# A fixed order for the value and sum matmuls of a fused attention and MoE kernel

## The chip, the cores and the metric

The kernel runs on one core of one Trainium2 chip. The metric is device time in microseconds (us). The kernel before has a median of 995.36 us over three runs (995.13 to 997.5).

## The reference, cut to what matters

```python
scores = scale * q @ k.T                       # batch 4, 8 heads, 768 positions, 64 wide
scores = where(mask, scores, -1e9)             # neighbours, first and last block, 3 sampled blocks
attn = exp(scores - max(scores))               # per row
attn = attn / (sum(attn) + 1e-9)
x = (attn @ v) -> [3072 tokens, 512]           # 8 heads side by side
h = x @ w_in                                   # 512 -> 2048
g = where(h >= 1, h, where(h <= -1, 0, (h + 1)**2 / 4))
out = g @ w_out                                # 2048 -> 512
```

Everything is float32, and the two weights arrive as 64-bit numbers.

## The kernel before, in words

The work is cut into 32 visits (one head of one batch each) and into MoE passes over half a batch (384 tokens), 16 steps of 128 hidden units per pass. A visit works on 6 column blocks `c` of 128 keys and two halves `hf` of 384 queries:

- `max_mm` (L285): 12 matmuls that recompute the scores once in one pass to find each row's maximum. DVE reduces each result (`max_red`, L291), takes the larger of two (L296), and PE transposes the column of maxima into a row (`max_turn`, L302, 6 small matmuls). ACT writes the row, negated, into row 96 of the query tile (`max_row`, L307), so that the score matmul subtracts it.
- `scores` (L323, L324): per block and half two matmuls into one PSUM bank; ACT takes the exponential (`expo`, L328) into a tile `pt`.
- `values` (L345): 12 matmuls of `pt` with `lv`. Each is a full float32 matmul, which the trace shows as two instructions. Its output is 64 rows wide: the half `hf` says whether it lands in rows 0 to 63 or 64 to 127 of the bank, so two neighbours use different halves of the array's columns.
- the row sums. In the first batch, whose visits the code calls `wide`, PE makes them: `p_tot` (L368), 12 float32 matmuls with a matrix of ones, 32 rows wide, in four column strips; ACT copies them out (L376) and they go through DRAM (`r_in`, `r_den`, `recip`) to come back as `den` for `x_mul` (L412). In the later batches POOL adds the tiles up (`p_sum`, L337), and `acc_sum` (L358) reduces them on DVE.
- `x_hi`, `x_lo` (ACT L224, DVE L422) split x into two reduced-precision parts for the MoE.

A MoE step is 12 matmuls `l1` (L487 to L489), an activation chain over ACT and DVE, and 9 matmuls `l2` (L521 to L523). The MoE of a batch starts when its 8 heads are done, and is mixed with the attention of the next batch. In the first 300 us or so the weights are converted as well: 16 conversions, each an ACT operation, four DVE operations over 1024 columns (L197 to L202), and two ACT casts with two DVE subtractions (L209).

What sets the order: every operation is entered into a list with a due time (`at`), in units of which one visit has 12 and with offsets from the tables `P`, `PW` and `PM`. The list is sorted and recorded in that order. The framework's scheduler then makes each engine's program from the recorded operations: it keeps the dependencies, but an instruction may stand before or behind one that was recorded earlier. Each engine executes its program strictly in order. SP issues nearly all transfers, in its own order.

Buffers: PSUM ring `pa` has three banks, used by `max_mm` (and by the scores of the later batches); scores of the first batch rotate over `oa0`, `oa1` and `hp`; 14 `pt` tiles; two sets of query and key tiles.

Of the kernel before, what the change touches and what calls it, by code (L numbers as in the profile page):

```python
# [38 lines left out]
def body(ctx, tc, qk_t, v, sampled_blocks, moe_w_in, moe_w_out, ind, cm, ident, fold, out):  # L39
    nc = tc.nc  # L40
    pool = lambda name, bufs, **kw: ctx.enter_context(tc.tile_pool(name=name, bufs=bufs, **kw))
    cst = pool("cst", 1)
    ld = pool("ld", 1)
# [6 lines left out]
    mt = pool("mt", 2)  # L50
# [98 lines left out]
    def after(key, *needs):  # L149
        assert all(x in passed for x in needs), (key, needs)  # L150
        passed.add(key)

    def at(t, fn, *args):
        plan.append((t, fn, args))

    turns = {}

# [15 lines left out]
    def plan_conversions():  # L173
        last = 1e9
        for t, load, bits, splits in sorted(conv, key=lambda x: -x[0]):
            last = t = min(t, last - P["cd"] * 2)
            at(t - P["cl"], load)
            at(t, bits)
            for i, split in enumerate(splits):
                at(t + P["cs"] + i * P["cg"], split)  # L180

    def convert(t, src, parts):
        st = {}

        def load():
            st["raw"] = cv.tile([128, 1024, 2], I32, name="raw", bufs=2)
            w = 1024 // len(src)
            for n in range(len(src)):
                Q_RAW.dma_start(out=st["raw"][:, n * w:(n + 1) * w],
                                in_=src[n].bitcast(I32).rearrange("p (c w) -> p c w", w=2))  # L190

        def bits():
            raw = st["raw"]
            lo32, hi32 = raw[:, :, 0], raw[:, :, 1]
            a = st["a"] = cv.tile([128, 1024], I32, name="cva", bufs=2)
            nc.scalar.activation(out=f(a), in_=f(hi32), func=AF.Abs)
            nc.vector.tensor_scalar(out=f(a), in0=f(a), scalar1=CLO, scalar2=CHI, op0=ALU.max, op1=ALU.min)  # L197
            nc.vector.tensor_scalar(out=a, in0=a, scalar1=3, scalar2=0x3FFFFFFF,
                                    op0=ALU.logical_shift_left, op1=ALU.bitwise_and)
            nc.vector.scalar_tensor_tensor(out=a, in0=hi32, scalar=-0x40000000, in1=a,  # L200
                                           op0=ALU.bitwise_and, op1=ALU.bitwise_or)
            nc.vector.scalar_tensor_tensor(out=a, in0=lo32, scalar=29, in1=a,  # L202
                                           op0=ALU.logical_shift_right, op1=ALU.bitwise_or)

        def split(cols, dst, done):
            a = f(st["a"])[:, cols]
            hi, lo = dst()
            rounded(CH, hi, a)
            nc.vector.tensor_tensor(out=lo, in0=a, in1=f(hi), op=ALU.subtract)  # L209
            done()  # L210

        conv.append((t, load, bits, [lambda x=x: split(*x) for x in parts]))
# [13 lines left out]
    def visit(n, b, h, pst):  # L226
# [3 lines left out]
        wide = n < H  # L230
        G = {**P, **PW} if wide else {**P, **PA} if n < 2 * H else P
        o0 = (L, R)[e]
# [77 lines left out]
        for m, (t, kh) in enumerate(jobs):  # L310
            u = n0 - (G["m0"] - G["m1"] * m / len(jobs))
# [118 lines left out]
                    at(s + G["ps"], p_sum, hf, c)  # L430
        for g in range(T // VG):
            u = n0 + 2 * (g + 1) * VG - 1 + G["lag"]
            at(u, values, g)
        for hf in range(2):
            at(u + G["ot"], o_copy, hf)
        if wide:
            at(u + 0.01, p_tot)
            at(u + G["al"], p_row)
            if e:
                y = u + G["su"]  # L440
                at(y, r_in)
                at(y + G["de"], r_den)
        else:
            at(n0 + 2 * T - 1 + G["al"] + G["ps"], acc_sum)
# [17 lines left out]
    def moe(t0, p, b, hf, fis, new=()):  # L462

        g = {}
        G = {**P, **PM} if new else P
        first, final = fis[0] == 0, fis[-1] == NF - 1
# [5 lines left out]
        def w_dst(fi):  # L472
            w = g["w", fi] = wst.tile([128, 2, DM], F32R, name="w")
            return w[:, 0], w[:, 1]

        def w_keep(fi):
            Q_KEEP.dma_start(out=f(wo_dram[fi]), in_=f(g["w", fi].rearrange("p a d -> p (a d)")))
# [75 lines left out]
        for i, fi in enumerate(fis):  # L553
            u = t0 + i * p
            if fi in new:
                if fi % 2 == 0:
                    convert(u + 1.5 * p - P["co"], [moe_w_out[k * 128:(k + 1) * 128, :] for k in (fi, fi + 1)],
                            [(slice((k - fi) * 512, (k - fi) * 512 + 512), lambda k=k: w_dst(k), lambda k=k: (w_keep(k), after(("wo", k))))
# [22 lines left out]
    at(-97, mask)  # L581
    at(-PW["qs"] + 0.1, mask_copies)
    at(-PW["qs"] + 0.15, mask_rest)
    for n in range(B * H):
        b, h = divmod(n, H)
        if h % 2 == 0:
            pst = {}
        visit(n, b, h, pst)
    full = tuple(range(NF))
    low, high = full[:NF // 2], full[NF // 2:]  # L590
    t = PER * H + D0
    for hf, fis, new in ((0, low, low), (1, full, high), (0, high, ())):
        moe(t, STEP0, 0, hf, fis, new)
        t += STEP0 * len(fis)
    for k in range(2, 2 * B):
        moe(PER * H * (1 + k / 2) + DELAY, PER * H / 2 / NF, k // 2, k % 2, full)
    for q in range(4):
        for kp in range(2):
            cs = slice(q * 512, (q + 1) * 512)
            u = 2 * q + kp  # L600
            convert(PER * H + D0 + (u - 4) * CSTEP - CONV + (STEP0 * NF / 2 if u > 3 else 0), [moe_w_in[k * 128:(k + 1) * 128, cs] for k in (2 * kp, 2 * kp + 1)],
                    [(slice((k % 2) * 512, (k % 2) * 512 + 512), lambda k=k, cs=cs: (wi[:, k, 0, cs], wi[:, k, 1, cs]),
# [1 line left out]
    plan_conversions()  # L604
    plan.sort(key=lambda x: x[0])
    for _, fn, args in plan:
        fn(*args)


LV, PT, VG, XT = 3, 14, 6, 10  # L610
STEP0 = 2.598
D0 = 10.127
P = {'r2': 3.428, 'qs': 8.321, 'vs': 2.922, 'ld': 2.0, 'm0': 7.7, 'm1': 5.1, 'mr': 0.037, 'mc': 2.3, 'mt': 1.061, 'mw': 0.459, 'ex': 0.5, 'ps': 0.823, 'lag': 0.994, 'ot': 0.4, 'al': 0.6, 'su': -0.02, 'de': 0.459, 're': 0.77, 'xm': -0.138, 'xh': 0.6, 'xl': 1.0, 'gr': 0.1, 'gs': 0.28, 'gm': 0.31, 'gh': 0.98, 'gl': 1.16, 'l2': 1.5, 'l3': 0.153, 'l1': 0.128, 'cl': 8.824, 'cs': 1.971, 'cd': 1.02, 'co': 5.155, 'cg': 1.066}
PW = {'qs': 9.6, 'vs': 4.0, 'ld': 4.0, 'm0': 9.0, 'm1': 8.0, 'mr': 0.3, 'mc': 0.9, 'mt': 0.6, 'mw': 0.373, 'ex': 0.6, 'ps': 1.084, 'lag': 1.153, 'ot': 0.4, 'al': 0.827, 'su': 1.75, 'de': 4.297, 're': 4.434, 'r2': 3.0, 'xm': -2.06, 'xh': 0.635, 'xl': 1.0}
PA = {}
PM = {'gr': -0.015, 'gs': 0.186, 'gm': 0.437, 'gh': 1.095, 'gl': 1.403, 'l2': 1.518, 'l3': 0.158, 'l1': 0.13}
RINGS = {"s": ("oa0", "oa1", "hp"), "m": ("pa", "pa")}
DELAY = 6.457
SETS = 2
PER = 2 * T  # L620
CONV = 4.0
CSTEP = 5.599
CLO, CHI = (struct.unpack("<f", struct.pack("<I", w))[0] for w in (0x38100000, 0x47EFFFFF))

_INS = ["qk_t", "v", "sampled_blocks", "moe_w_in", "moe_w_out"]
# [47 lines left out]
```

## Time and profile before

| | before |
|---|---|
| median of 3 runs | 995.36 us |
| profiled execution | 997.67 us |
| its span, first to last instruction | 995.9 us |
| PE busy | 971.9 us, 98% |
| PE weight loads busy | 764.5 us, 77% |
| DVE, ACT, POOL busy | 540.6, 527.9, 257.5 us |

The profiled execution is 2.3 us above the median, and 1.8 us longer than its span. Matmuls are pipelined: in the trace one lasts longer than the distance to the next, so the table's 98% says that PE always had something in flight, not that it ran at its shortest distances.

### The profile page before, as it was taken

How to read it: one execution, taken by the hardware profiler on the slowest of the kernel's cores; microseconds unless marked ns; L12 is line 12 of the kernel's file. 1: busy time of each engine (PE TensorE's matmuls, PEld its weight loads, DVE VectorE, ACT ScalarE, POOL GpSimd, SP SyncE). 2: the span in 40 equal slices, each digit the busy share in tenths (PEclk: the TensorE clock that was granted, in tenths of full speed). 3: DMA queues.
4: the chain of work that ended last, by engine and by line, in shares of the span. 5: the costliest groups of instructions: out<-in, count | busy, mean ns of one | idle time of the engine just before them, and what ended most of it. 6: DMA issues, size and time to landing. Idle time of an engine off the chain costs nothing.

```text
span 995.9 us, 13899 instructions
## 1 busy us (share of the span) xinstructions
PE 971.9 (98%) x5018; PEld 764.5 (77%) x5018; DVE 540.6 (54%) x918; ACT 527.9 (53%) x1043; POOL 257.5 (26%) x253
## 2 busy tenths in 40 slices
PE   5999999999999999999999999999999999999998
PEld 2444544578878898688888888888888888899997
DVE  5666754599878655654545556554545553322222
ACT  3546644557656555455555555555555545433433
POOL 1000000534332432533333344333333344000000
PEclk9999999999999999999999999999999999999999
DMA  6655664457774555545555545555555523433432
GB/s 210 166 157 166 164 183 136 118 182 249 236 221 134 163 179 171 162 136 156 154 153 163 160 124 150 166 151 156 157 152 166 149 86 101 154 127 127 159 126 96
DMA packets 53941, 155.99 MB, mean 157 GB/s; under 512 B 9130, under 2 KB 13386, under 8 KB 53872
## 3 DMA queue, kind: packets, MB, share of 16 engines
q1 hardware_dynamic: 53768, 154.93, 52.3%
q8 instruction: 40, 0.66, 0.3%
q14 instruction: 29, 0.24, 0.1%
q10 hardware_dynamic: 104, 0.17, 0.1%
HBM read 101.70 MB, written 15.61 MB: 118 GB/s over the span
## 4 chain that ended last, share of the span: by engine, by line
PE 88%; DVE 5%; DMA 4%; ACT 2%; issue 1%; SPq 0%; ACTq 0%
PE po L345 12%; PE oa L521 8%; PE oa L522 8%; PE oa L523 8%; PE hp L487 7%; PE hp L488 7%; PE hp L489 7%; PE pa L285 7%; PE pa L323 5%; PE pa L324 5%; PE oa L345 3%; DMA qk<-in_qk_t_dram 2%; DVE mc L291 2%; PE oa L323 2%; PE oa L368 1%; PE oa L324 1%
## 5 line engine op out<-in xcount | busy, mean ns | idle before, releaser
L337 POOL TENSOR_TENSOR acc<-acc,pt 128x384 f32<-128x384 f32 x192 | 201.2, 1049 | 217.4 <-ACT pt L328 214.5
L291 DVE TENSOR_REDUCE mc<-pa 128x1 f32<-128x384 f32 x384 | 203.4, 552 | 83.4 <-PE pa L285 77.4
L328 ACT ACTIVATE pt<-pa 128x384 f32<-128x384 f32 x288 | 140.5, 491 | 129.8 <-PE pa L324 121.6
L502 DVE SCALAR_TENSOR_TENSOR r<-r,hp 128x384 f32<-128x384 f32 x112 | 61.7, 551 | 203.7 <-ACT r L498 203.7
L487 PE MATMUL hp<-x,wi 128*128 128x384 f32 x448 | 153.0, 342 | 0.8 <-DVE r L502 0.7
L521 PE MATMUL oa<-w,gh 128*128 128x512 f32 x384 | 151.5, 395 | 0.3 <-ACT gh L224 0.3
L488 PE MATMUL hp<-x,wi 128*128 128x384 f32 x448 | 151.6, 338 | 0.0
L523 PE MATMUL oa<-w,gl 128*128 128x512 f32 x384 | 151.6, 395 | 0.0
L522 PE MATMUL oa<-w,gh 128*128 128x512 f32 x384 | 151.4, 394 | 0.0
L489 PE MATMUL hp<-x,wi 128*128 128x384 f32 x448 | 150.9, 337 | 0.0
L337 POOL TENSOR_TENSOR acc<-pt 128x384 f32<-128x384 f32 x48 | 52.6, 1097 | 360.0 <-ACT pt L328 196.8
L345 PE MATMUL po<-pt,lv 128*64 128x384 f32 x672 | 133.0, 496 | 0.0
L285 PE MATMUL pa<-KA,QA 88*128 88x384 f32 x384 | 128.8, 364 | 4.1 <-DMA QA<-qkh 2.2
L513 DVE TENSOR_TENSOR gl<-r,gh 128x384 fp32r<-128x384 f32 x128 | 89.7, 700 | 50.1 <-ACT gh L224 49.2
L494 ACT ACTIVATE r<-hp,half_c 128x384 f32<-128x384 f32 x112 | 65.0, 580 | 73.3 <-PE hp L489 71.9
L323 PE MATMUL pa<-QA,KA 97*128 97x384 f32 x288 | 101.8, 353 | 1.7 <-DVE mc L291 0.7
L285 PEld LDWEIGHTS pa<-KA,QA 88*128 88x128 f32 x384 | 71.3, 192 | 38.8 <-DVE mc L291 27.6
L324 PE MATMUL pa<-QB,KB 128*128 128x384 f32 x288 | 97.7, 339 | 0.0
L345 PEld LDWEIGHTS po<-pt,lv 128*64 128x64 f32 x672 | 55.3, 137 | 47.6 <-issue 40.1
L487 PEld LDWEIGHTS hp<-x,wi 128*128 128x128 f32 x448 | 84.6, 189 | 7.1 <-DVE r L502 3.9
L224 ACT CAST gh<-r 128x384 fp32r<-128x384 f32 x128 | 65.7, 513 | 40.8 <-DVE r L502 40.2
L488 PEld LDWEIGHTS hp<-x,wi 128*128 128x128 f32 x448 | 84.4, 188 | 1.8 <-DVE x L422 0.9
(85 smaller groups left out, 1222.4 us busy)
## 6 DMA issues: line engine op xcount, KB each, us to landing
w<-wo_dram SPq DMA_DIRECT2D x112, 512.0 KB
qk<-in_qk_t_dram SPq DMA_DIRECT2D x32, 384.0 KB
raw<-in_moe_w_in_dram SPq DMA_DIRECT2D x16, 512.0 KB
raw<-in_moe_w_out_dram SPq DMA_DIRECT2D x16, 512.0 KB
wo_dram<-w SPq DMA_DIRECT2D x16, 512.0 KB
lv<-in_v_dram SPq DMA_DIRECT2D x32, 192.0 KB
KA<-qkh SPq DMA_DIRECT2D x32, 192.0 KB
QA<-qkh SPq DMA_DIRECT2D x32, 192.0 KB
```

The lines of the kernel that those rows point to most:

```text
L285: nc.tensor.matmul(out=pm[:, 0:HALF], lhsT=QAi[0:KM, t * 128:(t + 1) * 128], rhs=KAi[0:KM, kh * HALF:(kh + 1) * HALF], start=True, stop=True)
L291: nc.vector.reduce_max(out=st["mc"][:, t, kh:kh + 1], in_=st.pop(("pm", t, kh))[:, 0:HALF], axis=AX.X)
L323: nc.tensor.matmul(out=ps[:, 0:HALF], lhsT=KAi[0:97, ks], rhs=QAi[0:97, cs], start=True, stop=False)
L324: nc.tensor.matmul(out=ps[:, 0:HALF], lhsT=st["KB"][:, ks], rhs=st["QB"][:, cs], start=False, stop=True)
L337: nc.gpsimd.tensor_tensor(out=st["acc"][:, hf], in0=prev, in1=st["p", hf, c], op=ALU.add)
L345: nc.tensor.matmul(out=st["po"][(L, R)[hf], 0:HALF], lhsT=st["lv"][:, c], rhs=st["p", hf, c], start=(c == 0), stop=(c == T - 1))
L487: nc.tensor.matmul(out=hv, lhsT=wi[:, j, 0, fs], rhs=x[:, 0], start=(j == 0), stop=False)
L488: nc.tensor.matmul(out=hv, lhsT=wi[:, j, 0, fs], rhs=x[:, 1], start=False, stop=False)
L489: nc.tensor.matmul(out=hv, lhsT=wi[:, j, 1, fs], rhs=x[:, 0], start=False, stop=(j == NP - 1))
L521: nc.tensor.matmul(out=o, lhsT=gh[:, ts], rhs=w[:, 0], start=(fi == fis[0]), stop=False)
L522: nc.tensor.matmul(out=o, lhsT=gh[:, ts], rhs=w[:, 1], start=False, stop=False)
L523: nc.tensor.matmul(out=o, lhsT=gl[:, ts], rhs=w[:, 0], start=False, stop=(fi == fis[-1]))
```

## The change

Three helpers are added. `behind` gives the scheduler an order without a semaphore: this instruction after that one. `fenced` records a function, chains all its PE instructions one behind the other, and puts the first behind the last 6 PE instructions recorded before. `traced` puts the first 10 PE instructions recorded behind a fenced group after that group's last. `values` and `p_tot` are now recorded through `fenced`, and all due times are new: the loads and splits of a first-batch visit (`qs`) are due 12.35 units ahead instead of 9.6, its maxima (`m0`) 10.5 instead of 9.

```diff
+    def behind(i, first):
+        tc.add_manual_dep(i, first.name, mybir.DependencyInfo(mybir.DependencyClass.NoSync, ...
+    def fenced(fn, *args):
+        k = len(nc.cur_bb.bb.instructions)
+        last = pe_from(-200)[-BEFORE:] if BEFORE else []
+        fn(*args)
+        new = pe_from(k)
+        for i in last:
+            behind(new[0], i)
+        for a, b in zip(new, new[1:]):
+            behind(b, a)
+        fence[:] = [new[-1], AFTER]
...
-            at(u, values, g)
+            at(u, fenced, values, g)
...
-            at(u + 0.01, p_tot)
+            at(u + G["tt"], fenced, p_tot)
...
-        fn(*args)
+        traced(fn, *args)
...
-PW = {'qs': 9.6, 'vs': 4.0, 'ld': 4.0, 'm0': 9.0, 'm1': 8.0, ...
+BEFORE, AFTER = 6, 10
+PW = {'qs': 12.353, 'vs': 6.524, 'ld': 3.794, 'm0': 10.499, 'm1': 10.933, ...
```

The same instructions are executed; only their order changes. Line numbers above 200 are 28 higher in the changed kernel: L345 becomes L373, L368 becomes L396, L285 becomes L313.

The first place is PE at the end of the fourth visit of the first batch: max matmuls (L285) of the next visit, values into `oa` (L345), sums (L368), the turn (L302), and the next visit's scores (L323, L324). Before:

```order
L285 MATMUL pa<-KA_112,QA_110 128x384
L345 MATMUL oa_839<-pt,lv 64x384
L285 MATMUL pa<-KA_112,QA_110 128x384
L345 MATMUL oa_839<-pt,lv 64x384
L285 MATMUL pa<-KA_112,QA_110 128x384
L345 MATMUL oa_839<-pt,lv 64x384 x2
L285 MATMUL pa<-KA_112,QA_110 128x384 x2
L345 MATMUL oa_839<-pt,lv 64x384
L368 MATMUL oa_852<-pt,ones 32x384 x9
L302 MATMUL pa<-idr,mr 1x128 x6
L368 MATMUL oa_852<-pt,ones 32x384 x3
L323 MATMUL oa_836<-QA_110,KA_112 128x384
```

The rest of the twelve values stands further up, also in pieces of one and two. The same place in the changed kernel:

```order
L351 MATMUL hp<-QA_111,KA_113 128x384
L313 MATMUL pa<-KA_112,QA_110 128x384
L352 MATMUL hp<-QB,KB 128x384
L313 MATMUL pa<-KA_112,QA_110 128x384 x3
L373 MATMUL oa_825<-pt,lv 64x384 x12
L396 MATMUL oa_839<-pt,ones 32x384 x12
L330 MATMUL pa<-idr,mr 1x128 x6
L351 MATMUL oa_868<-QA_110,KA_112 128x384
L352 MATMUL oa_868<-QB,KB 128x384
```

All maxima of the next visit now stand before the values, the values and the sums are one piece each, and the turn stands between the sums and the scores that need its row. From the third visit on it is alike for every visit of the first batch. Counted over the first eight visits, the values stand in 56 pieces before and in 8 after, the sums in 25 and in 8. In the later batches 21 of 24 visits had their values in one or two pieces before already; the three that had more are the ninth (8 pieces), the tenth (3) and the seventeenth (7).

The second place is DVE where the first batch's last normalisation (L412) stands, beside the reduction of POOL's sums of the ninth visit (L358). Before:

```order
L291 TENSOR_REDUCE mc<-pa 128x1 x12
L296 TENSOR_TENSOR mr<-mc 128x6
L412 TENSOR_TENSOR xun<-xun,den 128x768
L422 TENSOR_TENSOR x<-xun,x 128x384 x2
L358 TENSOR_REDUCE PS_115<-acc 128x24
L502 SCALAR_TENSOR_TENSOR r<-r,hp 128x384
```

DVE normalises first, and waits for POOL's sums behind it. In the changed kernel:

```order
L319 TENSOR_REDUCE mc<-pa 128x1 x5
L286 TENSOR_TENSOR qk<-qk,qkh 128x768
L324 TENSOR_TENSOR mr<-mc 128x6
L386 TENSOR_REDUCE PS_115<-acc 128x24
L440 TENSOR_TENSOR xun<-xun,den 128x768
```

The reduction of POOL's sums now stands ahead of the normalisation. On PE the first `l1` matmul that needs this x (L515, the tenth `l1` matmul of the program) stands behind nine of the ninth visit's values; before it stood behind all twelve. Changed:

```order
L330 MATMUL pa<-idr,mr 1x128 x6
L351 MATMUL pa<-QA_110,KA_112 128x384
L352 MATMUL pa<-QB,KB 128x384
L351 MATMUL pa<-QA_111,KA_113 128x384
L352 MATMUL pa<-QB,KB 128x384
L373 MATMUL po<-pt,lv 64x384 x9
L515 MATMUL hp<-x,wi 128x384
L373 MATMUL po<-pt,lv 64x384 x2
```

Here the group of values was not kept whole: three `l1` matmuls stand inside it.

## Rows read from the trace of the kernel before

**Rows 1.** The page: busy time by engine; weight loads' busy tenths in 40 slices.

```profile
PE 971.9 (98%) x5018; PEld 764.5 (77%) x5018; DVE 540.6 (54%) x918; ACT 527.9 (53%) x1043; POOL 257.5 (26%) x253
...
PEld 2444544578878898688888888888888888899997
```

**Rows 2.** Windows: stretch, length, busy us (instructions) per engine, clock, DMA share, GB/s.

```profile
18.00:168.00 150.00, 147.37 (x719) 70.96 (x720) 93.98 (x161) 81.49 (x168) 0.00 (x0) 0.99 0.58 165
...
200.00:400.00 200.00, 196.99 (x1037) 167.18 (x1036) 151.26 (x233) 122.00 (x238) 71.16 (x64) 1.00 0.60 190
850.00:950.00 100.00, 100.00 (x501) 90.26 (x500) 28.21 (x51) 41.84 (x79) 0.00 (x0) 1.00 0.45 145
```

**Rows 3.** Windows of L345 alone (values): PE, weight loads, clock, DMA.

```profile
18.00:168.00 150.00, 53.98 (x192) 12.89 (x192) 0.99 0.58 165
168.00:196.00 28.00, 9.27 (x30) 2.27 (x30) 1.00 0.44 111
...
430.00:850.00 420.00, 61.95 (x360) 30.89 (x360) 1.00 0.51 146
```

**Rows 4.** The same window of L368 alone (sums).

```profile
18.00:168.00 150.00, 26.85 (x192) 5.92 (x192) 0.99 0.58 165
```

**Rows 5.** PE timeline, fourth visit: start, us, instruction; a piece's x counts instructions.

```profile
85.64 0.34 PE L285 MATMUL pa<-KA,QA 88*128 88x384 f32 x1
85.91 0.87 PE L345 MATMUL oa<-pt,lv 128*64 128x384 f32 x4
86.70 0.62 PE L285 MATMUL pa<-KA,QA 88*128 88x384 f32 x2
87.16 0.34 PE L323 MATMUL hp<-QA,KA 97*128 97x384 f32 x1
...
88.95 0.86 PE L345 MATMUL oa<-pt,lv 128*64 128x384 f32 x2
89.74 0.45 PE L285 MATMUL pa<-KA,QA 88*128 88x384 f32 x1
```

**Rows 6.** PE timeline, a later visit with its values in one piece.

```profile
508.92 4.09 PE L345 MATMUL po<-pt,lv 128*64 128x384 f32 x24
512.94 0.44 PE L323 MATMUL pa<-QA,KA 97*128 97x384 f32 x1
```

**Rows 7.** PE timeline, sums and turn of the fourth visit.

```profile
93.41 2.12 PE L368 MATMUL oa<-pt,ones 128*32 128x384 f32 x18
95.46 0.52 PE L302 MATMUL pa<-idr,mr 128*1 128x128 f32 x6
95.91 0.85 PE L368 MATMUL oa<-pt,ones 128*32 128x384 f32 x6
96.68 0.44 PE L323 MATMUL oa<-QA,KA 97*128 97x384 f32 x1
```

**Rows 8.** ACT timeline beside it: the row of maxima, the copy of the sums.

```profile
95.83 0.85 ACT L307 ACTIVATE QA<-pa 1x384 fp32r<-1x384 f32 x2 [0.51 <-PE pa L302]
96.81 0.48 ACT L376 COPY acc<-oa 128x384 f32<-128x384 f32 x1
```

**Rows 9.** DVE groups from 18 to 168 us: busy us, mean ns, idle before them.

```profile
L291 DVE TENSOR_REDUCE mc<-pa 128x1 f32<-128x384 f32 x91 | 47.0, 552 | 34.5 <-PE pa L285 34.2
L200 DVE SCALAR_TENSOR_TENSOR cva<-raw,cva 128x1024 int32<-128x1024 int32 x7 | 8.5, 1221 | 0.1
...
L258 DVE TENSOR_TENSOR qk<-qk,qkh 128x768 f32<-128x768 f32 x8 | 7.7, 956 | 3.7 <-ACT qkh L224 3.7
...
L197 DVE TENSOR_SCALAR cva<-cva 128x1024 f32<-128x1024 f32 x7 | 4.8, 692 | 7.1 <-ACT cva L196 7.1
```

**Rows 10.** POOL group of the whole span.

```profile
L337 POOL TENSOR_TENSOR acc<-acc,pt 128x384 f32<-128x384 f32 x192 | 201.2, 1049 | 217.4 <-ACT pt L328 214.5
```

**Rows 11.** PE timeline: a values piece near the start, and a pause.

```profile
21.99 1.54 PE L345 MATMUL po<-pt,lv 128*64 128x384 f32 x2
23.46 0.69 PE L323 MATMUL oa<-QA,KA 97*128 97x384 f32 x1
...
42.47 0.44 PE L323 MATMUL oa<-QA,KA 97*128 97x384 f32 x1 [1.58 <-ACT QA L307]
```

**Rows 12.** Windows behind that pause.

```profile
42.00:44.00 2.00, 1.53 (x6) 1.49 (x6) 2.00 (x2) 1.98 (x4) 0.00 (x0) 0.72 0.47 100
44.00:46.00 2.00, 2.00 (x5) 0.79 (x4) 1.96 (x5) 1.78 (x6) 0.00 (x0) 0.50 0.95 249
```

More of the change, by code (lines that the diff above doesn't have):

```diff
@@ L154, in at, with pe_from, traced @@
         plan.append((t, fn, args))
+    fence = [None, 0]
+    def pe_from(k):
+        return [i for i in nc.cur_bb.bb.instructions[k:] if i.engine == mybir.EngineType.PE]
+    def behind(i, first):
+        tc.add_manual_dep(i, first.name, mybir.DependencyInfo(mybir.DependencyClass.NoSync, mybir.DependencyReason.DATA),
+                          reason="order")
+    def fenced(fn, *args):
[8 more added lines that the diff above has]
+        fence[:] = [new[-1], AFTER]
+    def traced(fn, *args):
+        k = len(nc.cur_bb.bb.instructions)
+        fn(*args)
+        if fence[1] and fn is not fenced:
+            for i in pe_from(k):
+                behind(i, fence[0])
+                fence[1] = max(0, fence[1] - 1)
     turns = {}
@@ L606, in body @@
     for _, fn, args in plan:
-        fn(*args)
+        traced(fn, *args)
 LV, PT, VG, XT = 3, 14, 6, 10
[L611 to L614, printed above, removed]
+BEFORE, AFTER = 6, 10
+STEP0 = 2.772
+D0 = 10.14
+P = {'r2': 3.428, 'qs': 8.723, 'vs': 6.261, 'ld': 2.0, 'm0': 7.841, 'm1': 5.1, 'mr': 0.431, 'mc': 2.3, 'mt': 1.032, 'mw': 0.604, 'ex': 0.317, 'ps': 0.804, 'lag': 1.492, 'ot': 2.579, 'al': 0.067, 'su': -0.02, 'de': 0.459, 're': 0.547, 'xm': -0.138, 'xh': 0.6, 'xl': 1.0, 'gr': 0.1, 'gs': 0.28, 'gm': 0.31, 'gh': 0.851, 'gl': 1.44, 'l2': 1.5, 'l3': 0.153, 'l1': 0.108, 'cl': 9.063, 'cs': 1.878, 'cd': 0.89, 'co': 5.29, 'cg': 2.287}
+PW = {'qs': 12.353, 'vs': 6.524, 'ld': 3.794, 'm0': 10.499, 'm1': 10.933, 'mr': 0.163, 'mc': 0.12, 'mt': 0.1, 'mw': 0.04, 'ex': 0.6, 'ps': 0.106, 'lag': 0.665, 'tt': 0.1, 'ot': 0.2, 'al': 0.572, 'su': 1.486, 'de': 4.3, 're': 4.4, 'r2': 2.866, 'xm': -2.402, 'xh': 0.576, 'xl': 1.0}
 PA = {}
-PM = {'gr': -0.015, 'gs': 0.186, 'gm': 0.437, 'gh': 1.095, 'gl': 1.403, 'l2': 1.518, 'l3': 0.158, 'l1': 0.13}
+PM = {'gr': -0.292, 'gs': 0.201, 'gm': 0.243, 'gh': 1.095, 'gl': 1.847, 'l2': 1.523, 'l3': 0.148, 'l1': 0.015}
 RINGS = {"s": ("oa0", "oa1", "hp"), "m": ("pa", "pa")}
-DELAY = 6.457
+DELAY = 5.905
 SETS = 2
 PER = 2 * T
-CONV = 4.0
-CSTEP = 5.599
+CONV = 3.972
+CSTEP = 3.374
 CLO, CHI = (struct.unpack("<f", struct.pack("<I", w))[0] for w in (0x38100000, 0x47EFFFFF))
```

## The prediction, made before the result was known

> **What bounds the kernel now.** I read the totals first: PE is busy 98% of the span, every other engine about half or less [rows 1]. Taken alone that says that there is nothing to win on PE. The weight loads say otherwise: in their 40 slices they are at 4 to 5 tenths through the first fifth and at 8 to 9 later [rows 1]. So I cut the span by stage. From 18 to 168 us, the eight visits of the first batch, PE counts as busy 147.4 of 150 us, its weight loads only 71.0; from 850 to 950 us, where only MoE matmuls run, it is 100.0 and 90.3 [rows 2]. The engine is occupied in the first stage, but starts less work.
>
> The Trainium skill, Perfetto Trace Analysis, "Identifying the Most-Contended Engine", says that matmul busy time is a poor measure of headroom and that the weight loads' share is a good one. By busy time this change could win at most 24 us in all, and next to nothing in this stage; by the loads' share the stage has room. The next rows decide it without the rule.
>
> In one piece, the 24 instructions of a visit's values take 4.02 us from their start to the next matmul's [rows 6]. In the first batch they come in pieces, and a piece of four takes 0.79 us from its start to the next one's, a piece of two also 0.79 (85.91 to 86.70, 88.95 to 89.74) [rows 5]. A single matmul thus pays for its missing neighbour in the other half of the columns. Nothing is waited for there: the rows show no idle time and no releaser. So the first stage is bound by PE through the shape of its order, and the stages behind it by PE with its matmuls near their shortest distance: from 200 to 400 us PE is busy 197.0 of 200 us with 167.2 of loads [rows 2].
>
> **The sum, against the profiled execution's 997.67 us (span 995.9 us).**
>
> Values, first batch. They are busy 53.98 us [rows 3]; each of the 56 pieces runs some 0.07 us into the next matmul (0.86 against 0.79 [rows 5]), so 53.98 - 56 x 0.07 = 50.1 us. In one piece each: 8 x 4.02 = 32.2. **-17.9 us.**
>
> Sums, first batch. 26.85 us busy [rows 4] in 25 pieces, less 25 x 0.07: 25.1. How long 24 in one piece take is not in the trace. Eighteen take 2.05 us and six 0.77 [rows 7]; with four column strips, 18 are three rounds of eight, the last not full, and 24 are three full rounds, so I take 2.05 as well. Bounds: 2.05 and 2.05 + 0.77 = 2.82. 8 x 2.05 = 16.4. **-8.7 us** (-2.5 by the upper bound).
>
> Edges. One max matmul ahead of a piece takes 0.27 us instead of 0.18 (85.64 to 85.91), two behind it 0.46 instead of 0.35 (86.70 to 87.16) [rows 5]: about 0.2 us per piece, 81 x 0.2 = 16. Afterwards a visit has an edge into the values, one from the values to the sums (another column width), and one out, for which I allow 0.75 us together, 8 x 0.75 = 6. **-10 us.**
>
> The Trainium skill, TensorEngine Tiling (Array Packing), "Key Properties", says that changing the tiling mode drains the engine. By that rule alone only the number of switches counts, and the sum would hold the 10 us of edges. The rows show a second cost that the rule lacks, the piece of two that costs as much as one of four [rows 5]; the measurement decides, and both stand in the sum.
>
> Ninth, tenth and seventeenth visit. 30 instructions in 10 pieces take 9.27 - 10 x 0.07 = 8.6 us [rows 3] where 30 at 4.02/24 take 5.0, and their edges 10 x 0.2, of which the new group keeps some: -5. The seventeenth has 7 pieces, about 6 x 0.79 + 0.2 x 6 against 4.02: -2. **-7 us.** Elsewhere the values are whole already: 61.95 us for 360 [rows 3] is 4.13 per visit.
>
> Gross: 17.9 + 8.7 + 10 + 7 = 43.6 us.
>
> What comes in its place. (1) The turn now stands behind all sums, directly ahead of the scores that need its row. Before, six instructions of sums (0.77 us) covered the ACT row operation [rows 7, 8]. Now ACT must copy the sums first (0.48 us [rows 8]) and then write the first half of the row, about 0.45 us: scores start about 1.1 us behind the sums, of which the turn itself fills 0.45. 8 x 0.65 = 5.2, less the pauses of this kind that exist already (the 1.58 us at 42.47 [rows 11]): **+3.5.** (2) The twelve maxima must all be done before the values. DVE reduces them at 47.0/91 = 0.52 us each [rows 9], with three banks, so the last may start no sooner than nine reductions behind the first. The first three stand behind some ten score matmuls: 1.1 + 10 x 0.177 + 0.35 + 9 x 0.52 = 7.9 us after the sums, where matmuls alone need 1.1 + 36 x 0.177 = 7.5. With the two DVE operations that stand among the reductions I take 0.65 per visit: **+5.** (3) The first visit has no scores to lay beside the next one's maxima: 12 x 0.52 - 12 x 0.177 = +4, and in the second visit a conversion stands ahead of the reductions, +2: **+6.** (4) Entry into the MoE: POOL's ten additions for the ninth visit last 10 x 1.05 us [rows 10] and start about 2 us behind the first batch's last sums; the reduction, the normalisation and the ACT cast follow, so the first matmul on that x is ready at some 15 us, while PE arrives at about 36 x 0.177 + 0.65 + 0.45 + 0.35 + 9/12 x 4.02 = 11 to 12 us: **+4.** Bounds for (1) to (4) together: 0, if planned work fills all of it, and twice the 18.5 us.
>
> Loads planned further ahead I cost at nothing: in the first stage PE's idle time is 2.6 us in all [rows 2], so no transfer was holding it up much; what they cost, if they now delay a raw weight load, would show as DVE waiting, and is in the first rival.
>
> Net: 43.6 - 18.5 = 25 us, 997.67 - 25 = 972.6. The profiled execution lies 2.3 us above the median of the runs, so the time to be measured is 972.6 - 2.3, about **970 us.**
>
> **Rivals.** *The feeding engines take most of it.* A visit with one conversion asks of DVE 12 x 0.52 + (2 x 1.22 + 4 x 0.69) + 0.96 [rows 9], where the conversion's other operations are taken like the two shown, and some 1.2 for the rest: 13.6 us, against a visit of 14 to 15 us on PE; DVE also waited 7.1 us ahead of its conversions [rows 9]. Seven conversions fall into a stage that is 20 us shorter. For: nearly full, in strict order. Against: it was busy only 94.0 of 150 us [rows 2]. Price: 2 us in each of five visits and 4 more at the MoE's entry: 984.
>
> *Nothing new is waited for.* The reductions, the row and the MoE's entry hide behind scores: 997.67 - 43.6 - 2.3 = 952. For: the order was dense before. Against: strict order and the row that scores need.
>
> *The pieces filled waits that come back whole.* Then the visit's period stays what ACT and DVE set, 995. Against: ACT was busy 81.5 of 150 us [rows 2].
>
> *Slower: the lower clock.* After the 1.58 us pause at 42.47 us the granted clock is 0.72 and then 0.50 for two stretches of 2 us, 1.2 GHz [rows 12]; near the start a values piece of two took 1.47 us instead of 0.79 [rows 11], behind twelve maxima spaced by DVE. If maxima that wait for DVE, and the pause for the row, bring the lower clock in every visit, values and sums run at half speed: +6.1 us a visit, 8 x 6.1 = 49, 970 + 49 = 1019. It decides from five visits on (5 x 6.1 = 30 > 25). Against: most of these pauses are below 1 us, and the stage has a mean of 0.99 [rows 2].
>
> **How the numbers follow.** The forecast has a chance of 0.58, with its own range 962 to 978 (half of 18.5 us either way); feeding engines 0.20 (984), nothing new 0.12 (952), waits come back 0.04 (995), lower clock 0.06 (1019). The range is to leave out the last two and the far end of the bounds: 950 to 987. A measurement of this kernel tells 0.3%, 3 us, from no change. Faster: 0.58 + 0.20 + 0.12 = 0.90; the same 0.04; slower 0.06.
>
> **What would show it.** Right: values at 8 x 4.1 us and sums at 8 x 2.1 busy in the first batch; its last sums end near 145 us, where the stage reached to 168 before; the weight loads' tenths rise from 4 to 5 or 6 in the first slices; the stages behind 430 us unchanged in length. (1) shows as PE idle ahead of L351 released by ACT's row, (2) as maxima spaced about 0.5 us, (4) as idle ahead of L515 released by DVE. Wrong: DVE busy over 90% from 20 to 145 us, a granted clock near 0.5 in values, or a stage from 150 to 400 us that grows by what the first one lost.

## The result, and the profile after

The changed kernel takes 970.14 us (median of 4 runs, 968.96 to 972.12) against 995.99 us for the kernel before beside it (4 runs): ratio 0.9741, interval 0.9718 to 0.9764. The forecast was 970. Its profiled execution takes 972.12 us with a span of 970.3, where the one before had 997.67 and 995.9.

Lines moved by 28: values are L373, sums L396, maxima L313, turn L330, row L335, scores L351 and L352, first `l1` matmul L515. From the page of the changed kernel, the totals, the weight loads' slices and the clock's (as [rows 1]):

```profile
PE 941.3 (97%) x5018; PEld 770.0 (79%) x5018; DVE 528.3 (54%) x918; ACT 514.0 (53%) x1043; POOL 258.4 (27%) x253
...
PEld 3546564878888888788888888788888888899997
...
PEclk9899999999999999999999999999999999999999
```

The low tenths of the weight loads end after seven slices and rise within the first batch to 5 and 6. The windows by stage (PE, weight loads, DVE, ACT, POOL, clock, DMA; as [rows 2]):

```profile
18.00:148.00 130.00, 122.31 (x734) 77.41 (x733) 94.42 (x167) 84.76 (x171) 0.00 (x0) 0.97 0.70 199
200.00:400.00 200.00, 197.39 (x1049) 167.24 (x1047) 143.15 (x228) 119.24 (x239) 78.36 (x70) 1.00 0.62 190
850.00:950.00 100.00, 100.00 (x503) 90.60 (x502) 26.35 (x48) 39.88 (x75) 0.00 (x0) 1.00 0.40 135
```

The first batch ends 20 us sooner: its last sums, 24 in one piece, start at 145.39 and the next matmul at 147.46 us, where that matmul stood at 167.24 before. More of that stage is idle now: 130 - 122.3 = 7.7 us, where [rows 2] had 2.6 of 150. The stages behind are nearly as they were: from the tenth turn to the last instruction 809.7 us before (995.9 - 186.21) and 811.3 now (970.3 - 159.00). The same window for values alone (L373), then for sums alone (L396), as [rows 3, 4]:

```profile
18.00:148.00 130.00, 35.37 (x192) 13.91 (x192) 0.97 0.70 199
```

```profile
18.00:148.00 130.00, 17.14 (x192) 5.41 (x192) 0.97 0.70 199
```

Values fell from 53.98 to 35.37 us, sums from 26.85 to 17.14. On the PE timeline, a visit's values in one piece (4.02 us to the sums behind them), then what stands behind the seventh visit's values:

```profile
94.40 4.09 PE L373 MATMUL po<-pt,lv 128*64 128x384 f32 x24
...
128.14 2.14 PE L396 MATMUL oa<-pt,ones 128*32 128x384 f32 x24
130.21 0.52 PE L330 MATMUL pa<-idr,mr 128*1 128x128 f32 x6
131.38 0.45 PE L351 MATMUL oa<-QA,KA 97*128 97x384 f32 x1 [0.65 <-ACT QA L335]
```

Twenty-four sums take 2.07 us where eighteen took 2.05 [rows 7], which fits three rounds with the last one not full. Behind the turn PE waits 0.65 us for ACT's row. The chief waits of PE from 18 to 200 us (us in all, times, longest):

```profile
PE oa L351 <- ACT QA L335: 3.5, 6, 0.7
PE pa L330 <- DVE mr L324: 1.9, 2, 1.7
PE hp L351 <- ACT QA L335: 1.8, 2, 1.2
PE oa L351 <- ACT pt L356: 1.2, 3, 0.6
PE pa L313 <- ACT pt L356: 0.9, 3, 0.4
PE pa L313 <- DVE mc L319: 0.4, 2, 0.2
```

Two places run at the lower clock. In the first visit, on the PE timeline and in the windows beside it:

```profile
28.13 4.40 PE L313 MATMUL pa<-KA,QA 88*128 88x384 f32 x9 [0.19 <-DVE mc L319]
32.46 6.73 PE L373 MATMUL po<-pt,lv 128*64 128x384 f32 x24
39.12 2.14 PE L396 MATMUL oa<-pt,ones 128*32 128x384 f32 x24
```

```profile
32.00:34.00 2.00, 2.00 (x8) 0.86 (x9) 2.00 (x6) 0.00 (x0) 0.00 (x0) 0.50 0.00 0
...
38.00:40.00 2.00, 2.00 (x20) 0.70 (x20) 2.00 (x3) 0.72 (x2) 0.00 (x0) 1.00 0.02 4
```

Behind nine maxima, one per DVE reduction (4.33/9 = 0.48 us apart), the granted clock is 0.50, 1.2 GHz, and the values take 6.66 us instead of 4.02. The visit's scores ahead of these maxima are slow as well: 24.08 to 24.40, 0.32 us from one to the next, where matmuls of this width stand 0.18 apart later. The windows give 1.00 for the clock there; 0.32 us is the distance that such scores have where the clock is given as 0.50 (153.61 to 153.93 in the run with both mended places below). And at the entry into the MoE, PE and then DVE:

```profile
159.00 0.52 PE L330 MATMUL pa<-idr,mr 128*1 128x128 f32 x6 [1.71 <-DVE mr L324]
...
160.46 5.13 PE L373 MATMUL po<-pt,lv 128*64 128x384 f32 x18
165.52 0.45 PE L515 MATMUL hp<-x,wi 128*128 128x384 f32 x1
```

```profile
157.03 0.96 DVE L286 TENSOR_TENSOR qk<-qk,qkh 128x768 f32<-128x768 f32 x1
157.91 0.95 DVE L324 TENSOR_TENSOR mr<-mc 128x6 fp32r<-128x6 f32 x1
161.92 0.98 DVE L386 TRANSPOSE_TENSOR_REDUCE PS<-acc 128x24 f32<-128x768 f32 x1 [3.06 <-POOL acc L365]
162.82 0.92 DVE L440 TENSOR_TENSOR xun<-xun,den 128x768 f32<-128x768 f32 x1
```

The turn waits 1.71 us for DVE's column, and the 18 values behind it take 5.06 us instead of 18 x 4.02/24 = 3.0. The `l1` matmul itself waits for nothing.

### The profile page after: what moved, and what is told of

It reads as the page before. It is cut to its first block, busy times and chain, and to the rows that moved or that the text cites. A ratio compares the mean times of both kernels' runs of the same rounds, so it can differ in the third digit from the quotient of the medians.

```text
span 970.3 us, 13907 instructions
## 1 busy us (share of the span) xinstructions
PE 941.3 (97%) x5018; PEld 770.0 (79%) x5018; DVE 528.3 (54%) x918; ACT 514.0 (53%) x1043; POOL 258.4 (27%) x253
## 4 chain that ended last, share of the span: by engine, by line
PE 83%; DVE 7%; DMA 4%; ACT 4%; issue 1%; SPq 1%; POOL 0%; DVEq 0%; ACTq 0%; POOLq 0%
PE po L373 11%; PE oa L549 8%; PE oa L551 8%; PE oa L550 8%; PE hp L515 8%; PE hp L516 7%; PE hp L517 7%; PE pa L313 6%; PE pa L351 5%; PE pa L352 5%; DVE mc L319 2%; DMA qk<-in_qk_t_dram 2%; PE oa L373 1%; PE pa L517 1%; PE pa L516 1%; PE pa L515 1%
## 5 line engine op out<-in xcount | busy, mean ns | idle before, releaser
L365 POOL TENSOR_TENSOR acc<-acc,pt 128x384 f32<-128x384 f32 x192 | 203.3, 1060 | 204.0 <-ACT pt L356 202.7
L319 DVE TENSOR_REDUCE mc<-pa 128x1 f32<-128x384 f32 x384 | 198.0, 551 | 70.3 <-PE pa L313 65.5
L515 PE MATMUL hp<-x,wi 128*128 128x384 f32 x448 | 154.2, 344 | 1.1 <-ACT x L252 0.6
L313 PE MATMUL pa<-KA,QA 88*128 88x384 f32 x384 | 129.1, 365 | 6.4 <-DMA QA<-qkh 2.4
L373 PE MATMUL po<-pt,lv 128*64 128x384 f32 x672 | 120.8, 505 | 0.0
L541 DVE TENSOR_TENSOR gl<-r,gh 128x384 fp32r<-128x384 f32 x128 | 77.4, 604 | 51.6 <-ACT gh L252 50.7
L351 PE MATMUL pa<-QA,KA 97*128 97x384 f32 x288 | 100.2, 348 | 0.5 <-ACT pt L356 0.2
L352 PE MATMUL pa<-QB,KB 128*128 128x384 f32 x288 | 97.6, 339 | 0.0
L515 PEld LDWEIGHTS hp<-x,wi 128*128 128x128 f32 x448 | 84.4, 188 | 15.8 <-issue 9.6
L313 PEld LDWEIGHTS pa<-KA,QA 88*128 88x128 f32 x384 | 73.9, 194 | 28.3 <-DVE mc L319 13.1
L373 PEld LDWEIGHTS po<-pt,lv 128*64 128x64 f32 x672 | 56.8, 141 | 49.2 <-issue 41.8
```

The lines of the kernel that those rows point to most:

```text
L313: nc.tensor.matmul(out=pm[:, 0:HALF], lhsT=QAi[0:KM, t * 128:(t + 1) * 128], rhs=KAi[0:KM, kh * HALF:(kh + 1) * HALF], start=True, stop=True)
L319: nc.vector.reduce_max(out=st["mc"][:, t, kh:kh + 1], in_=st.pop(("pm", t, kh))[:, 0:HALF], axis=AX.X)
L351: nc.tensor.matmul(out=ps[:, 0:HALF], lhsT=KAi[0:97, ks], rhs=QAi[0:97, cs], start=True, stop=False)
L352: nc.tensor.matmul(out=ps[:, 0:HALF], lhsT=st["KB"][:, ks], rhs=st["QB"][:, cs], start=False, stop=True)
L365: nc.gpsimd.tensor_tensor(out=st["acc"][:, hf], in0=prev, in1=st["p", hf, c], op=ALU.add)
L373: nc.tensor.matmul(out=st["po"][(L, R)[hf], 0:HALF], lhsT=st["lv"][:, c], rhs=st["p", hf, c], start=(c == 0), stop=(c == T - 1))
```

## The experiments

Two theories to begin with: *pieces*, that the fenced groups bring the gain, as the prediction has it; *due times*, that it comes from the new tables. Each half was then run alone.

### The fences alone

```diff
-PW = {'qs': 12.353, ..., 'mc': 0.12, 'mt': 0.1, 'mw': 0.04, ..., 'lag': 0.665, 'tt': 0.1, ...}
+PW = {'qs': 9.6, ..., 'mc': 0.9, 'mt': 0.6, 'mw': 0.373, ..., 'lag': 1.153, 'tt': 0.01, ...}
```

(and the other tables as before.)

> The kernel before with the fences added, and its own due times kept (the sums 0.01 units behind the values). Values stand in 32 pieces, sums in 8, for all visits. Theory 'pieces' (the gain is the matmuls no longer paying for missing neighbours and edges): values busy 33 us in the first batch and sums 17, time 968 to 980, at least 16 of the 26 us. Rival 'due times' (loading and splitting further ahead is what lets PE run densely): the pieces' 36 us come back as PE waiting for DVE and ACT in the first batch, time 988 or more.

Measured 1009.87 us, ratio 1.0139 (1.012 to 1.0158): 1.4% slower, clear of the noise. The groups are whole, yet nothing is won. The window, the wait and a visit on the PE timeline:

```profile
18.00:174.00 156.00, 132.65 (x738) 80.04 (x739) 94.00 (x168) 83.27 (x172) 0.00 (x0) 0.87 0.60 173
```

```profile
PE pa L330 <- DVE mr L324: 16.9, 9, 3.1
```

```profile
71.96 0.80 PE L330 MATMUL pa<-idr,mr 128*1 128x128 f32 x6 [3.08 <-DVE mr L324]
74.34 0.69 PE L351 MATMUL hp<-QA,KA 97*128 97x384 f32 x1 [1.58 <-ACT QA L335]
74.82 0.52 PE L352 MATMUL hp<-QB,KB 128*128 128x384 f32 x1
75.28 5.35 PE L373 MATMUL po<-pt,lv 128*64 128x384 f32 x24
```

Here the turn stands ahead of the values, so nothing lies between the last maxima and the column that DVE makes of them: 16.9 us of waiting in nine pauses, and in seven of the eight visits the lower clock takes part of the values behind (0.87 over the stage, 0.50 in the windows from 72 to 76 us): they take 5.08 to 6.74 us, 5.27 in the visit shown. This is the prediction's slower rival, at a lower price: the values are busy 44.48 us in this stage, (44.48 - 8 x 4.09)/8 = 1.5 us a visit too many, where the rival had 6.1 for values and sums. *Pieces* falls in its simple form.

### The due times alone

> The changed kernel's due times without the fences: the scheduler cuts values into 97 pieces (66 in the first 16 visits or so of the kernel before were its most) and sums into 13. Theory 'pieces': no gain, 990 to 1005. Rival 'due times': most of the gain stays, 975 or less.

Measured 998.79 us (ratio 1.0023, 1.0005 to 1.0041). Values stay in pieces: 52.50 us busy from 18 to 168 us. So *due times* falls too: neither half is worth anything alone.

### The turn's place

The first run with seven due times of the change, those that put a first-batch turn behind values and sums; loads, maxima and everything behind the batch as before.

```diff
-'mc': 0.9, 'mt': 0.6, 'mw': 0.373, 'lag': 1.153, 'tt': 0.01, 'ot': 0.4, 'al': 0.827
+'mc': 0.12, 'mt': 0.1, 'mw': 0.04, 'lag': 0.665, 'tt': 0.1, 'ot': 0.2, 'al': 0.572
```

> Fences alone came out slower than before: there the turn stands ahead of the last two score matmuls and of the values, so that PE waits for DVE's last maxima and for ACT's row with nothing to do, and the values behind it run at the lower clock. This kernel has the fences and the old due times (loads, splits and maxima no further ahead), but seven due times of the changed kernel that put column, turn and row behind values and sums. Theory 'place of the turn': nearly all of the gain, 970 to 980. Rival 'planned further ahead' (loads, splits and maxima due earlier are what is needed beside the fences): 990 or more.

Measured 984.73 us (ratio 0.9884, 0.9865 to 0.9903): 25 of the some 40 us that lie between the first run and the changed kernel, and a result between the two expectations. Starts of turns on the PE timelines say where:

| turn of visit | before | fences alone | turn behind | changed |
|---|---|---|---|---|
| 3 | 57.97 | 52.91 | 55.97 | 55.92 |
| 8 | 146.63 | 147.68 | 130.51 | 130.21 |
| 10 | 186.21 | 185.49 | 158.94 | 159.00 |
| 13 | 279.88 | 288.79 | 262.43 | 251.76 |
| 32 | 813.21 | 825.76 | 798.60 | 788.80 |

Up to the tenth turn this run is the changed kernel. It loses 10.7 us between the tenth and the thirteenth, as the fences alone do. There, at the MoE's entry:

```profile
164.26 0.69 PE L515 MATMUL hp<-x,wi 128*128 128x384 f32 x1 [4.39 <-ACT x L252]
...
165.79 6.25 PE L373 MATMUL po<-pt,lv 128*64 128x384 f32 x24
```

An `l1` matmul stands ahead of the ninth visit's values and waits 4.39 us for x; the values behind it run at the lower clock, 6.18 us. That is 6.5 us, some 4.5 more than the changed kernel loses behind its tenth turn. By the count of matmuls started, the run is 4.7 us behind the changed kernel at 200 us, 7.1 at 230 and still 7.0 at 400, but 12.7 at 430. The second step is the same thing once more, at the second batch's entry into the MoE:

```profile
401.18 0.44 PE L515 MATMUL hp<-x,wi 128*128 128x384 f32 x1 [1.14 <-ACT x L252]
```

From there to 405.44 PE waits 2.7 us in four pauses, and the granted clock is 0.50 from 404 to 408; in the changed kernel no pause there exceeds 0.34 us and the clock stays at 1.00.

### Loads and maxima not ahead

The changed kernel with five due times as before.

```diff
-'qs': 12.353, 'vs': 6.524, 'ld': 3.794, 'm0': 10.499, 'm1': 10.933
+'qs': 9.6, 'vs': 4.0, 'ld': 4.0, 'm0': 9.0, 'm1': 8.0
```

> The changed kernel with five due times of the first batch as they were before: loads of queries, keys and values and the two due times of the maxima (qs, vs, ld, m0, m1); the fences, the place of the turn and everything behind the first batch as in the change. If planning the first batch's loads and maxima further ahead is worth nothing, as the prediction costed it: 968 to 972 us, first batch's last sums again near 147.5 us, and what the run with seven due times lacked (984.7 against 970) comes from the MoE's entry and the border between the batches. If the loads ahead bring it: 980 to 985, with waits for DMA or for DVE's reductions ahead of the first batch's maxima.

Measured 971.64 us (ratio 0.9759, 0.9737 to 0.9782), not told from the changed kernel's 970.14. In the first batch the old due times do cost something: in the trace the scores at 73.02 wait 2.15 us for the row, the granted clock is 0.50 behind that (76 to 80 us), and the eighth turn starts at 133.80, 3.6 us later than in the changed kernel. By the last turn this is gone (788.44 against 788.80); the ninth visit's values, for one, take 5.02 us instead of 6.65. So the first batch planned further ahead is worth next to nothing in the whole, and the due times matter through the turn and through what they set behind the first batch. Which of those, the MoE's or the weight conversions', no run separates; the trace shows the price at the MoE's two entries.

### What a neighbour is worth

The first batch's values in whole groups, six of one column half and then six of the other.

```diff
+cols = range(g * VG, (g + 1) * VG)
-for c in range(g * VG, (g + 1) * VG):
-    for hf in range(2):
+for c, hf in [(c, hf) for hf in range(2) for c in cols] if wide else [(c, hf) for c in cols for hf in range(2)]:
```

> The changed kernel, but in the first batch a group's twelve value matmuls are issued six for the one column half and then six for the other, so that neighbours lie in the same half. Same matmuls, same unbroken group. Theory 'a matmul pays for its missing neighbour': a single one costs 0.65 us, a visit 12 x 0.65 = 7.7 us instead of 4.0, 8 x 3.7 = 30 us more: about 1000. Rival 'edges only' (a piece costs by its switches in and out, not by what stands in it): no change, 970.

Measured 991.31 us in one run. On the PE timeline:

```profile
51.33 6.72 PE L374 MATMUL oa<-pt,lv 128*64 128x384 f32 x24
57.98 2.14 PE L397 MATMUL oa<-pt,ones 128*32 128x384 f32 x24
```

6.65 us for the same 24 instructions in seven visits, and 8.34 instead of 6.66 in the first: 7 x (6.65 - 4.02) + 1.7 = 20.1, and the profiled executions differ by 991.31 - 972.12 = 19.2. The order alone makes this difference, which bears out that neighbours in different halves run beside each other. Neighbours of the same half also add into the same output rows; the two score matmuls of a block do so, too (88.46 and 88.63 in the changed kernel), at 0.18 us each, so that is no likely cause, but no run separates it for the values. My price per visit was too high, since a piece's 0.79 us [rows 5] holds an edge too.

### Values fenced in the first batch only

```diff
-at(u, fenced, values, g)
+at(u, *([fenced, values] if wide else [values]), g)
```

> The changed kernel with the values fenced in the first batch only: the ninth, tenth and seventeenth visits' values stand in pieces again (16 more pieces in all). Theory 'pieces': 16 pieces at 0.2 us of edges and some 4 us of missing neighbours come back, 975 to 977. Rival (there the pieces fill the wait for the first batch's last x and cost nothing): 970.

Measured 974.34 us (968.93 to 979.11; ratio 0.9758, 0.9724 to 0.9792). With a spread of 10 us it can't tell 970 from 976.

### The changed kernel again

> The changed kernel itself, as the yardstick for the runs beside it: 968 to 972.

Measured 969.12 us (ratio 0.9725, 0.971 to 0.974).

### The turn between values and sums

```diff
-'mc': 0.12, 'mt': 0.1
+'mc': 0.3, 'mt': 0.28
```

> The changed kernel with the turn (and the column it needs) due between values and sums. The row then is written while the sums run: theory 'pause for the row' (0.65 us in each of eight visits, 5.3 us of PE idle ahead of L351): 965, 4 to 5 us less. Rival (the pause hides a wait for exponentials or reductions that comes anyway): 969 to 971.

Measured 974.05 us (ratio 0.9772, 0.9751 to 0.9792): 4.9 us more than the changed kernel beside it (969.12), which neither expectation had. The profiled execution is the shortest of the five (970.01 us, mean granted clock 0.995; the others 973.8 to 975.3 at 0.988 to 0.991), so its trace shows why nothing is won, not what the others lose. The waits for the row are gone (0.2 us left), and the fifth visit's values start 4.0 us sooner (90.4 against 94.4). But other waits stand in their place from 18 to 160 us, and ahead of the sixth visit's values nine maxima come at DVE's pace, with these values at 5.25 us; the ninth visit's values start 1.0 us later than in the changed kernel.

```profile
PE pa L313 <- DMA QA<-qkh: 2.7, 4, 1.1
PE pa L330 <- DVE mr L324: 2.6, 3, 1.2
PE oa L351 <- ACT acc L404: 0.9, 1, 0.9
```

```profile
104.57 4.41 PE L313 MATMUL pa<-KA,QA 88*128 88x384 f32 x9 [0.19 <-DVE mc L319]
```

### The clock in the first visit

Eleven more matmuls among the second visit's maxima; their results are overwritten.

```diff
+if n == 1 and (t, kh) >= (0, 1):
+    if (t, kh) == (0, 1):
+        st["fill"] = pso.tile([128, 512], F32, name="po")
+    nc.tensor.matmul(out=st["fill"][:, 0:HALF], ...)
```

> The changed kernel with eleven extra matmuls, whose result is overwritten, among the second visit's maxima, which DVE paces at half a microsecond each. In the changed kernel the granted clock falls to 0.50 there and the first visit's values take 6.7 us instead of 4.0. Theory 'PE at work keeps the clock up': values 4.0 us, 967. Rival (the clock falls by what the scores before it do, or the extra matmuls delay the maxima): 970 to 972.

Measured 968.64 us (ratio 0.9716, 0.9699 to 0.9732), not told from 969.12. In its trace the clock stays at 1.00 from 28 to 40 us. On the PE timeline (the last maxima, values, sums):

```profile
30.38 1.94 PE L313 MATMUL pa<-KA,QA 88*128 88x384 f32 x5
32.25 4.09 PE L379 MATMUL po<-pt,lv 128*64 128x384 f32 x24
36.27 2.14 PE L402 MATMUL oa<-pt,ones 128*32 128x384 f32 x24
```

The values now take 4.02 us. The second turn starts 2.9 us sooner than in the changed kernel (38.34 against 41.20), the eighth still 2.2, the eleventh 1.0: at the MoE's entry the granted clock is 0.50 from 154 to 162 us, longer than in the changed kernel (0.68 from 160 to 162, 0.50 to 164). That the extra matmuls keep the clock up is likely, not shown. In the two traces that have them the first visit's values take 4.02 us; in nine of the ten with whole groups and without them the clock falls there; but in the run with the turn between values and sums it does not, behind the same nine maxima 0.45 us apart, and the values take 4.02 us too:

```profile
27.88 4.16 PE L313 MATMUL pa<-KA,QA 88*128 88x384 f32 x9 [0.30 <-DVE mc L319]
```

### The MoE's entry

First the tenth visit's column ahead of the split on DVE; then, apart from it, the ninth visit's normalisation ahead of the reduction of POOL's sums; then the first of these with the eleven matmuls.

```diff
# first: seen["col"] is the tenth visit's column operation on DVE
+if n == H + 2: behind(own(DVE), seen["col"])      # the split beside it
# second: seen["norm"] is the ninth visit's normalisation
+if n == H: behind(own(DVE), seen["norm"])         # the reduction of POOL's sums
-at(n0 + 2 * T - 1 + G["al"] + G["ps"], acc_sum)
+at(n0 + 2 * T - 1 + G["al"] + G["ps"] + (3.0 if n == H else 0.0), acc_sum)
```

> The changed kernel with one DVE order turned round: for the tenth visit the column operation that its turn waits for (mr, 0.95 us) stands ahead of the split beside it. If the price of the MoE's entry sits at this turn (1.71 us from column to turn, then 18 matmuls of values at half clock, 5.13 us instead of about 3.0): the pause at 159.0 falls to about 0.8, the values keep the clock, 967 to 968.5 us. If the normalisation behind it sets the entry (POOL's additions until 161.9, the cast at 163.8, first l1 at 165.5): the values end sooner and l1 waits the more, 969 to 971 us.

> The changed kernel with the ninth visit's normalisation ahead of the reduction of POOL's sums on DVE, so that the MoE's first x is ready some 2 to 3 us sooner. If the first l1 matmul pays for POOL's sums and the normalisation, as step (4) of the prediction has it: 966 to 968 us, l1 earlier. If the wait sits at the turn and in the clock, where l1 had no idle time ahead of it in the changed kernel: 969 to 971 us.

> Both mended places in one kernel: eleven extra matmuls (their results are overwritten) among the second visit's maxima, and the tenth visit's column operation ahead of the split on DVE. If both groups of values keep the clock (4.1 us instead of 6.7, and 18 to 22 matmuls in about 4.1 instead of 5.1) and nothing behind takes it back: 2.6 + 1 to 2 us less than the changed kernel, 965.5 to 967.5 against 969 to 970. If the row behind the sums, DVE's reductions and the MoE's first x take it back: 968 to 970.

Measured: column first 970.88 us (966.47 to 975.34; ratio 0.9748, 0.9721 to 0.9775), normalisation first 969.89 (0.9731, 0.9717 to 0.9745), both mended places 970.39 (0.9731, 0.9717 to 0.9744). None is told from the changed kernel. With the column first, on the PE timeline:

```profile
156.24 0.52 PE L338 MATMUL pa<-idr,mr 128*1 128x128 f32 x6 [0.17 <-ACT pt L364]
...
157.71 4.08 PE L381 MATMUL po<-pt,lv 128*64 128x384 f32 x22
162.30 0.45 PE L523 MATMUL hp<-x,wi 128*128 128x384 f32 x1 [0.51 <-ACT x L256]
```

The 1.71 us are gone, so this price did sit at the turn, and the values keep the full clock; now `l1` waits for x. That the clock hangs on that pause is not shown: in the run with both places the pause is gone as well, but the clock is low ahead of the turn already (at 156.94 there), and 22 instructions of values take 5.00 us:

```profile
152.00:154.00 2.00, 1.74 (x6) 1.18 (x5) 1.46 (x4) 1.21 (x2) 1.38 (x2) 0.50 0.03 3
```

With the normalisation first, `l1` starts no sooner (166.84 against 165.52) and waits for nothing, as in the changed kernel.

With the column first the profiled execution has a span of 966.8, 3.5 us shorter than the changed kernel's; but 1.6 us of it stand at the eighth turn (128.62 against 130.21), ahead of the edit. Its six runs spread over 9 us, 966.5 to 969.6 at a mean granted clock of 0.998 and 972.2 to 975.3 at 0.993 and 0.994, and their median is no lower. In the run with both, the second turn starts 2.0 us sooner than in the changed kernel, the tenth 2.1 and the last 1.0; the changed kernel profiled again is at 787.37 with that last turn, 1.4 sooner than the first time without any edit. So two profiles of one kernel differ by more than what these edits save at the end, and no version better than the changed kernel was found.

## Why the prediction was right, step by step

The mechanism was right: matmuls without a neighbour in the other column half, and edges between kinds. The sum came out (25 us foreseen, 997.67 - 972.12 = 25.6 measured), and nearly step by step. I took the distance from each PE instruction's start to the next one's, less the idle time that the timeline records, and what it exceeds the shortest distance by (values 4.02/24, sums 2.05/24, others 0.177 us):

| step | foreseen | measured |
|---|---|---|
| values, first batch | -17.9 | 50.1 to 34.8 (35.37 - 8 x 0.07); 2.6 of the 34.8 are the first visit's lower clock, which belongs to (3): -17.9 |
| sums | -8.7 | 25.2 to 16.6: -8.6 |
| edges, first batch | -10 | scores and maxima directly beside a value, a sum or a turn, from the second turn to the ninth, exceed their shortest distance by 11.6 before, 1.8 after: -9.8 |
| ninth, tenth, seventeenth visit | -7 | values 17.5 to 14.7, of which 2.1 belong to (4): -4.9; edges from the ninth turn to the nineteenth 3.9 to 1.2: -2.7 |
| (1) row | +3.5 | waits for the row, second turn to tenth, 2.0 before, 5.1 after: +3.1 |
| (2) maxima | +5 | second turn to tenth: maxima right behind maxima exceed their shortest distance by 0.3 before, 3.1 after; idle ahead of maxima 0 before, 0.9 after: +3.7 |
| (3) start | +6 | first visit: maxima +2.1, scores +1.5, values +2.6: +6.2 |
| (4) entry | +4 | pause 1.71, values 2.1 over full speed: +3.8 |

The measured steps add up to -27.1. The 1.5 us between that and the trace lie mainly in what the prediction left out: the MoE's matmuls take 1.7 us more, other scores and maxima 2.5 more, other values 1.3 less, and the first matmul starts 0.9 sooner. A second profile of the changed kernel differs by 2.4 us from the first, so an agreement to 0.6 us in the whole is in part luck, and so are the sizes of (3) and (4), which came for another reason.

*Values and sums:* right, by the trace and by the run with neighbours in one half.

*Edges:* right. Before, 99 scores and maxima stand directly beside a piece from the second turn to the ninth and exceed their shortest distance by 0.12 us each; 13 are left. Scores and maxima now meet each other more often (118 times from the second turn to the tenth), but that costs 0.015 us each.

*(1):* right. 0.65 us per visit was foreseen, and 0.65 stands at 131.38; 5.3 us in eight waits, where three of 2.2 us in all stood before.

*(2):* too high, and only half of it is DVE. The idle time that the profile lists ahead of maxima is small, 0.4 us for DVE's reductions and 0.9 for ACT; most of the price lies in maxima that stand 0.3 to 0.5 us apart without a pause long enough to be listed. In the first batch that is 1.9 us, and in the ninth visit, where maxima and scores share their banks, another 1.8, there mostly for ACT's exponentials. On the PE timeline, the last maxima in the third visit, then a stretch of the eighth:

```profile
64.83 0.90 PE L313 MATMUL pa<-KA,QA 88*128 88x384 f32 x2 [0.22 <-DVE mc L319]
...
135.14 0.36 PE L313 MATMUL pa<-KA,QA 88*128 88x384 f32 x1
135.33 0.34 PE L352 MATMUL oa<-QB,KB 128*128 128x384 f32 x1
135.51 0.34 PE L351 MATMUL hp<-QA,KA 97*128 97x384 f32 x1
135.68 0.34 PE L313 MATMUL pa<-KA,QA 88*128 88x384 f32 x1
```

In the eighth, two scores stand between maxima, which are so 0.54 us apart, DVE's own pace (0.52). Most reductions are covered by work that was there anyway; the prediction had ten scores in front and the maxima bare behind them.

*(3):* the size held and the cause was a third right. DVE does pace the maxima, but that is 2.1 of the 6.2 us; the values' 2.6 are the lower clock, which the prediction kept for its slower rival, and the scores' 1.5 come at the distance that they have at the lower clock.

*(4):* the size held and the place was wrong. The prediction had PE waiting at `l1` for POOL's sums and the normalisation; it waited at the turn for a DVE column, and lost the rest to the clock; with the normalisation ahead, `l1` started no sooner. Where the old due times put `l1` ahead of the values, the wait stands where it was foreseen, 4.39 us.

*Loads at nothing:* held in the time, 971.64 against 970.14, though 3.6 us of the first batch hang on them for a while; and in the second profile of the changed kernel two of the row's pauses (0.65 and 1.21 us) are put down to a load. But "planned further ahead" was not all of the new due times. The prediction priced the turn's place only by the row's pause; the runs show that the fences gain nothing without that place: 1009.87 with the old turn, 984.73 with the new. The prediction took the changed order as given, so its sum held, but it would have named the fences alone as the cause.

*Rivals:* the feeding engines stayed far from full (DVE 94.4 of 130 us). The lower clock came in two visits, below the five from which it decides; in the run of the fences alone it came in seven of the first batch's eight, and that kernel is slower than the one before.

*The loads' share:* the Trainium skill, Perfetto Trace Analysis, "Identifying the Most-Contended Engine", on which the first reading leaned, holds that the weight loads' share shows the headroom better than matmul busy time. The traces agree: PE's busy share moved by one point (98% to 97%) while 25 us went, and the loads' share of the first stage rose from 71.0/150 = 47% to 77.4/130 = 60%.

## What to carry to other kernels

Fix the order of small matmuls into whole groups that alternate column halves, but look in the same step at what then stands ahead of each group: an operation that waits for another engine must have the group between itself and its producer. Where an order is strict, price a long pause twice, once for its own time and once for the matmuls behind it at the lower clock (it came behind the pauses of 1.71, 2.15 and 4.39 us shown here, not behind those of 0.65 to 1.19 in the changed kernel). And take a small gain away from one place only where the runs can tell it: here four mended pauses of 2 to 5 us each moved no median by 2 us for the better.

## What the runs showed of the hardware that was not expected

- Two neighbouring float32 matmuls with 64 columns of output in the same half cost 6.65 us per 24 instructions, in different halves 4.02: a factor of 1.65, not of 2.
- The lower clock came without much recorded idle time: behind nine maxima spaced by 0.48 us, with one pause of 0.19 us, the windows show 0.50 from 31 to 37 us; with eleven more matmuls among them the clock stayed at 1.00, but so it did once without them.
- DVE's column operation on 128 x 6 elements, 0.166 us in the median of 32, took 0.95 us at 157.91, where POOL had begun its additions at 157.54:

```profile
157.54 2.25 POOL L365 TENSOR_TENSOR acc<-acc,pt 128x384 f32<-128x384 f32 x2 [0.38 <-ACT pt L356]
```

  The first of the two additions ends at 158.83, the column at 158.86. In the run with the column first it stood at 155.93, as an addition of POOL ended, and took 0.17 us. All columns of the changed kernel that meet an addition go one of these two ways. Four start while an addition runs (157.91, 188.05, 220.40, 395.32), take 0.95 to 0.98 us, and end 0.02 to 0.03 us behind it; three start some 0.1 us ahead of an addition (248.68, 278.15, 337.73) and take 0.16. The Trainium skill, SBUF — State Buffer, "SBUF: two separate sides", says that DVE operations with two inputs in SBUF and GpSimd's share one pair of ports, which the one that starts first holds for its whole instruction; the seven places agree with that.
